# One weight load of a spectral transformer block, issued by ScalarE in the third group of the frequency stage instead of by SyncE

## The chip, the core and the metric

The kernel runs on one core of a Trainium2 chip. The core has a matrix engine (TensorE, PE in the profile; its weight loads are listed as PEld), a vector engine (VectorE, DVE), a scalar engine (ScalarE, ACT), a general engine (GpSimd, POOL) and a sequencer without arithmetic (SyncE, SP). Each works through its own list of instructions in order, and semaphores tie the lists together. Any of SP, ACT and POOL can issue a DMA; the transfer itself runs on 16 DMA engines and ends with a semaphore. The metric is the time of one execution in microseconds of device time. Shown is the median of several runs.

## What is computed

A block of 2048 tokens of width 640 with conditioning: a layer norm, scaled and shifted by parts of a modulation vector, goes through a two-dimensional Fourier filter; a second layer norm, scaled and shifted by other parts, goes through a gated feed-forward layer.

```python
mod = (_silu(c) @ w_mod).reshape(c.shape[0], 6, 1, -1)
sa, ca, ga, sb, cb, gb = (mod[:, 0].copy(), mod[:, 1].copy(), ...)
h = _layernorm(x, axis=-1) * (1 + ca) + sa
x = x + ga * _A_ref(h, A_w_r, A_w_i)          # rfft2, times (w_r + i w_i), irfft2
h = _layernorm(x, axis=-1) * (1 + cb) + sb
x = x + gb * _B_ref(h, B_w_gate, B_w_up, B_w_down)   # (silu(h Wg) * (h Wu)) Wd
```

`w_mod` has 640 rows and six column blocks of 640. The blocks for `sb` and `cb`, the shift and the scale of the second layer norm, are what this document is about: 1600 KB together.

## The kernel before

The order of the work on every engine is the order in which the program issues it; nothing is rearranged. Four parts follow one another.

First, to about 36 us, the tokens are transformed along the width and half way along the sequence, in 16 tiles of 128 tokens. In this part SP has some 20 loads in its list, the filter weights and their mirrored copies among them. Of `w_mod`, the blocks `ca` (L247, L249), `sa` (L275) and `ga` (L279) are loaded here.

Second comes the frequency stage, from about 37 to 63 us. The 81 kept frequencies of the width are worked on in 21 groups (`NG`) of two to four. For a group g,

- `stage_a(g)` makes one TensorE matmul for each frequency (L567) into two banks of PSUM, and VectorE multiplies the result by the filter weights in two instructions (L592, in `prod`);
- `stage_b(g)` sums the products with matmuls against the identity (L599) into bank 0 or 1, and ScalarE copies that bank out (L602);
- `stage_c(u)`, two or three groups later, transforms back (L620), and `evac` moves two groups' results out at a time, most of them by ScalarE (L637). GpSimd then makes a turned copy (L648).

The loop over g (L694) runs `stage_a(g + 2)`, `stage_b(g)` and `stage_c` of the unit that is due, in this order. The frequencies reach `stage_a` transposed. The first 18 (groups 0 to 4) are transposed by TensorE (`t2_pe`, L538). The others come by four DMA transposes (`t2_dma`, L519), issued by SP one after the other: for groups 5 to 8, 9 to 12, 13 to 16 and 17 to 20. Before the first group of such a batch is used, GpSimd adds a constant to it (`sa_add`, L559).

Right behind the four transposes, SP's list has the load of the blocks `sb` and `cb` (L527), the block `gb` (L528), two tables for the inverse transform (H, L529, and RI, L530), and the weights of the feed-forward layer from L734 on. In `w_mod`'s tile they are `wm_r[:, :, 1:3, :]` and `wm_r[:, :, 3, :]`.

What reads `sb` and `cb` is `mod_col` (L578 to L581): five matmuls of one output column each for one of the five 128-wide pieces of the width. They are strewn into `stage_a` of the last four groups, 17 to 20, behind the first matmul of the group (L568 to L570): two pieces in groups 17 and 18, three in 19 and 20. Each engine's list being in order, the other matmuls of these groups stand behind them. `gb` is read at the end of the stage (L718).

Third, to about 82 us, the inverse transform along the sequence and the width, with the residual and the statistics of the second norm (L669, L678, L1184 to L1189). It reads H and, scaled by `ga`, RI (L724, L728).

Fourth, the feed-forward layer in four chunks of tokens, from 82 us to the end (gate and up: L1013 and L1043; down: L891 and L914).

A DMA issue here also waits for the last DMA that used the same one of eight semaphores. For L527 that is the load of a table at L280, about 20 us earlier.

Of the kernel before, what the change touches and what calls it, by code (L numbers as in the profile page):

```python
# [149 lines left out]
def _rev(ap, free_off, dims):  # L150
    a = ap[:]
    return bass.AP(tensor=a.tensor, offset=a.offset + free_off, ap=[list(a.ap[0])] + [list(d) for d in dims])
# [3 lines left out]
def adaln_block_kernel(ctx, tc, A_x, A_w_r, A_w_i, B_x, B_w_gate, B_w_up, B_w_down, c, w_mod, out):  # L156
    nc = tc.nc
# [55 lines left out]
    wm_r = rM.cut(12800, [NC5, 4, D])  # L213
# [19 lines left out]
    def banks(b, n, shape=None, dt=F32):  # L233
        ap = psum[:, b:b + n, :].rearrange("p b e -> p (b e)")
        if dt == BF16:
            ap = ap.bitcast(BF16)
        if shape is not None:
            ap = ap[:, 0:int(np.prod(shape))]
            if len(shape) > 1:
                ap = ap.rearrange("p (a b) -> p a b", a=shape[0])  # L240
        return ap
# [36 lines left out]
    wm_m = wm_v[:, :, 2 * D:6 * D].rearrange("p k (i d) -> p k i d", i=4)  # L278
# [46 lines left out]
    if True:  # L325
# [76 lines left out]
        def wsum(W, lo, hi, eng):  # L402

            off = lo if W is Wn else NW - hi
            v = [_rev(W, NT * NW * i + off, [[NW, NT], [160, 2], [1, hi - lo]]) if W is Wn else
                 _rev(W, NT * NW * i + off - 160, [[NW, NT], [160, 2], [1, hi - lo]]) for i in range(3)]
            eng.tensor_tensor(v[1], v[2], v[0], ALU.add)
# [104 lines left out]
    if True:  # L512
        B2of = {}

        def t2_dma(bi):
            l0 = (1, 16, 32, 64)[bi]
            n = 15 if bi == 0 else 16
            B2b = rL.cut(4096 * bi, [16, 128]) if bi < 3 else rM.cut(6144, [16, 128])
            nc.sync.dma_start_transpose(B2b[:, :n, :], A_sb[:, l0:l0 + n, :, :, :].rearrange("p l t c r -> p l (t c r)"))  # L519
            for i in range(n):  # L520
                B2of[l0 + i] = (B2b, i, l0, n)
# [2 lines left out]
        t2_dma(1)  # L524
        t2_dma(2)
        t2_dma(3)
        nc.sync.dma_start(wm_r[:, :, 1:3, :], wm_m[:, :, 1:3, :])  # L527
        nc.sync.dma_start(wm_r[:, :, 3, :], wm_m[:, :, 3, :])  # L528
        nc.sync.dma_start(Htab[:], H_dram)  # L529
        nc.sync.dma_start(RI[:], RI_dram)  # L530
# [22 lines left out]
        def sa_add(g):  # L553
            if g < 5 or g >= NG:
                return
            B2b, i, l0, nb = B2of[groups[g][0]]
            if l0 not in seen:
                seen.add(l0)
                nc.gpsimd.tensor_tensor(B2b[:, :nb, 0:1], B2b[:, :nb, 0:1], SA[:, l0:l0 + nb].unsqueeze(2), ALU.add)  # L559

        def stage_a(g):
            ls = groups[g]
            n = len(ls)
            xps = banks(6 if g == 2 else 2 + 2 * (g % 2), 2, [4, 256])
            for i, l in enumerate(ls):
                B2, j = B2of[l][0:2]
                nc.tensor.matmul(xps[:, i, 0:192], lhsT=B2[:, j, :], rhs=KS2, start=True, stop=True)  # L567
                if i == 0:  # L568
                    for c5 in {NG - 4: (0, 1), NG - 3: (0, 1), NG - 2: (2, 3, 4), NG - 1: (2, 3, 4)}.get(g, ()):
                        mod_col(psum[:, 2 + 2 * (g % 2), 192 + c5:193 + c5], wm_r[:, :, 1 + g % 2], c5)  # L570
            PP = rM.cut(1536 * (g % 4), [3, 2, NT, 2, n])
            prod(g, PP, xps, 0)
            if g == 0:
                wsum(Wv, 48, 64, nc.vector)
            prod(g, PP, xps, 1)
            return PP

        def mod_col(o, w, c5):  # L578
            for k in range(NC5):
                nc.tensor.matmul(o, lhsT=w[:, k, 128 * c5:128 * c5 + 128], rhs=sc_col[:, k:k + 1],  # L580
                                 start=(k == 0), stop=(k == NC5 - 1))  # L581
# [12 lines left out]
        def stage_b(g, PP):  # L594
            n = len(groups[g])
            yps = banks((g + 1) % 2, 1, [4, 128])
            for ps in (1, 0):
                for i in range(n):
                    nc.tensor.matmul(yps[:, i, :], lhsT=_rev(PP, 64 * n * ps + i, [[n, 128]]), rhs=identb[:],  # L599
                                     start=(ps == 1 and i == 0), stop=(ps == 0 and i == n - 1))  # L600
            Y2 = rY.cut(1024 * (g % 4), [4, 128])
            nc.scalar.copy(Y2[:, 0:n, :], yps[:, 0:n, :])  # L602
            return Y2
# [8 lines left out]
        def stage_c(u):  # L612
            for g in units[u]:
                ls = groups[g]
                n, l0 = len(ls), ls[0]
                eps_ = banks({NG - 4: 4, NG - 3: 5, NG - 2: 0, NG - 1: 1}.get(g, 6 + (l0 // 4) % 2), 1, [4, 128])
                Y2 = Y2s.pop(g)
                for i, l in enumerate(ls):
                    kv = {0: 1, 80: 2}.get(l, 0)
                    nc.tensor.matmul(eps_[:, i + 4 - n if l0 else i, :], lhsT=Y2[:, i, :], rhs=Ktab[:, 128 * kv:128 * kv + 128],  # L620
                                     start=True, stop=True)

        def evac(u):
            g, l0 = units[u][0], groups[units[u][0]][0]
            if l0 == 0:
                edge = rY.cut(4096, [2, 128])
                nc.scalar.copy(edge[:], banks(6, 1, [4, 128])[:, 0:2, :])
                for i in range(2):
                    nc.gpsimd.tensor_copy(Em[:, :, :, 64 * i].rearrange("p v q -> p q v"),
                                          edge[:, i, :].rearrange("p (q v) -> p q v", v=2))  # L630
            elif g == NG - 2:
                nc.vector.tensor_copy(ep_views(l0, 4), banks(0, 1, [4, 128]).rearrange("p i q -> p q i"))
            elif g == NG - 1:
                nc.scalar.copy(ep_views(l0, 4), banks(1, 1, [4, 128]).rearrange("p i q -> p q i"))
            else:
                n = len(groups[g]) + 4
                (nc.vector.tensor_copy if g == NG - 6 else nc.scalar.copy)(  # L637
                    ep_views(l0, n), banks(4 if g == NG - 4 else 6, 2, [8, 128])[:, 8 - n:8, :].rearrange("p i q -> p q i"))
                if g < NG - 4:
                    rots.extend((l0, n, i) for i in range(0 if g == NG - 6 else 2))  # L640

        def rot(l0, n, qs, eng, ops=(0, 1)):
            if l0 < 64:
                E0, E1 = (Em[:, v].rearrange("p q (c j) -> p q c j", c=2)[:, qs, :, l0:l0 + n] for v in range(2))
            else:
                E0, E1 = (Er[:, v, qs, :, l0 - 64:l0 - 64 + n] for v in range(2))
            for i in ops:
                eng.tensor_scalar(E1[:, :, 1 - i, :], E0[:, :, i, :], 1.0 - 2.0 * i, 1.0, ALU.mult, ALU.mult)  # L648
# [45 lines left out]
        for g in range(NG + 1):  # L694
            if g > 1:
                sa_add(g + 4)
            for W, lo, hi in {0: ((Wv, 80, 81), (Wv, 0, 16)), 1: ((Wv, 16, 32),), 3: ((Wv, 32, 48),), 11: ((Wn, 64, 80),), 13: ((Wv, 64, 80),)}.get(g, ()):
                wsum(W, lo, hi, nc.gpsimd)
                if g == 0 and hi == 81:
                    sa_add(5)  # L700
            if 0 < g < NG - 2:
                PPs[g + 2] = stage_a(g + 2)
            if g == NG - 3:
                nc.vector.tensor_copy(modcols[:, 2, :], psum[:, 2, 192:197])
                nc.vector.tensor_scalar_add(one_p_cb[:], psum[:, 4, 192:197], 1.0)
            if rots:
                l0, n, i = rots.pop(0)
                rot(l0, n, slice(0, 64), nc.gpsimd, (i,))
            if g < NG:
                Y2s[g] = stage_b(g, PPs.pop(g))  # L710
            for u, gs in enumerate(units):
                if gs[-1] + (1 if gs[0] >= NG - 2 else 3 if gs[0] == 4 else 2) == g:
                    stage_c(u)
                    evac(u)
            if g == NG - 3:
                rot(40, 8, slice(0, 64), nc.vector)
            if g == NG - 1:
                for c5 in range(NC5):  # L718
                    mod_col(psum[:, 3, 192 + c5:193 + c5], wm_r[:, :, 3], c5)
# [602 lines left out]
```

## Time and profile before

| | |
|---|---|
| median of 3 runs | 248.64 us (248.44 to 250.56) |
| the profiled execution | 249.31 us, of which the span is 247.5 |
| granted TensorE clock | 1.00 |
| first part, 0 to 37 us: PE busy | 35.53 us |
| frequency stage, 37 to 63 us: PE, DVE, ACT busy | 24.97, 23.05, 21.62 us |
| inverse transform, 63 to 82 us: PE, DVE, ACT busy | 18.98, 16.94, 16.97 us |
| load of `sb` and `cb` (L527): issue, landing | 48.06 us, 7.3 us later |

The span is the time from the first to the last instruction of the profiled execution; the rest of its time lies around it. Busy times are those of instructions; the issue of a DMA is listed on the engine's sequencer (SPq, ACTq) and is not counted as busy. The number in brackets behind a line of a timeline is the idle time of the engine before it, and what ended it. Where several like instructions were merged into one row, the row gives their count and the time from the first one's start to the last one's end.

### The profile page before, as it was taken

The numbers are of one execution on the slowest core, as the hardware profiler recorded it, in microseconds if no ns is written. First come the engines' busy times: TensorE is split into PE (matmuls) and PEld (weight loads), VectorE is DVE, ScalarE is ACT, GpSimd is POOL, SyncE is SP. The second block draws the span as 40 slices with busy tenths as digits, with TensorE's granted clock in tenths as the row PEclk, the third lists the DMA queues.
The fourth block names the chain that finished last, engine by engine and source line by source line (L and its number), as shares of the span: only waits on it lengthen the run. The fifth ranks groups of instructions, "written<-read, shape, count | busy, mean of one in ns | idle before, by whom it ended". The sixth has DMA issues, their size and how long they took to land.

```text
span 247.5 us, 6173 instructions
## 1 busy us (share of the span) xinstructions
PE 241.5 (98%) x2327; PEld 189.7 (77%) x2327; DVE 207.7 (84%) x516; ACT 167.8 (68%) x327; POOL 78.1 (32%) x128
## 2 busy tenths in 40 slices
PE   8999999999999999999999999999999999999994
PEld 3778877989999888688887778887765666656773
DVE  3799699988898998789989977788998787789864
ACT  3778757996989698489774488866246777773220
POOL 8577765993243605002004400000432000004400
PEclk9999999999999999999999999999999999999999
DMA  7999999999999999600005110200411000000111
GB/s 220 396 361 315 307 391 177 179 337 392 295 348 317 298 280 187 139 15 3 0 3 106 53 55 3 57 0 19 93 49 53 3 0 1 4 0 0 53 56 53
DMA packets 45760, 34.74 MB, mean 140 GB/s; under 512 B 21732, under 2 KB 42659, under 8 KB 45347
## 3 DMA queue, kind: packets, MB, share of 16 engines
q1 hardware_dynamic: 43936, 30.00, 42.7%
q0 software_dynamic: 1504, 4.28, 7.4%
q8 instruction: 18, 0.29, 0.5%
q10 hardware_dynamic: 290, 0.08, 0.1%
q14 instruction: 12, 0.09, 0.1%
HBM read 27.05 MB, written 4.72 MB: 128 GB/s over the span
## 4 chain that ended last, share of the span: by engine, by line
PE 89%; DVE 4%; DMA 3%; issue 1%; ACT 0%; POOL 0%; DVEq 0%; SPq 0%; ACTq 0%; POOLq 0%
PE psum L1043 36%; PE psum L914 19%; PE psum L1013 6%; PE psum L891 3%; DMA rM<-in_w_mod_dram 3%; PE psum L669 3%; PE psum L599 2%; PE psum L296 2%; PE psum L1184 2%; PE psum L1187 2%; PE psum L1001 2%; PE psum L567 2%; DVE rE L382 2%; PE psum L318 1%; PE psum L315 1%; PE psum L393 1%
## 5 line engine op out<-in xcount | busy, mean ns | idle before, releaser
L1043 PEld LDWEIGHTS <-rW 128*128 128x128 bf16 (+1 forms) x429 | 42.0, 98 | 12.6
L1043 PE MATMUL psum<-rW 128*128 128x256 bf16 (+1 forms) x247 | 42.2, 287 | 0.0
L940 POOL TENSOR_TENSOR rM<-rM,rL 128x320 f32<-128x320 f32 x6 | 5.4, 906 | 96.6 <-ACT rL L939 96.6
L914 PEld LDWEIGHTS <-rE 128*128 128x128 f16 (+1 forms) x196 | 19.0, 97 | 7.8
L914 PE MATMUL psum<-rE 128*128 128x320 f16 (+1 forms) x147 | 22.9, 299 | 0.0
L592 DVE TENSOR_TENSOR rM<-psum,rW 128x384 bf16<-128x384 f32 (+2 forms) x42 | 20.2, 543 | 2.7 <-PE psum L567 1.2
L1074 ACT COPY rH<-psum 128x384 f32<-128x384 f32 (+2 forms) x27 | 14.0, 517 | 7.4 <-PE psum L1043 6.0
L1081 ACT COPY rX<-psum 128x384 f32<-128x384 f32 (+2 forms) x27 | 14.0, 520 | 7.2 <-PE psum L1043 7.0
L1043 PEld LDWEIGHTS <-rE 128*128 128x128 f16 x156 | 15.3, 98 | 4.7
L1078 DVE TENSOR_TENSOR rH<-psum,rM 128x512 bf16<-128x512 f32 (+1 forms) x24 | 15.0, 624 | 4.4 <-PE psum L1043 2.2
L1097 ACT ACTIVATE rL<-psum 128x384 bf16<-128x384 f32 (+2 forms) x27 | 14.4, 533 | 5.3 <-PE psum L1043 3.4
L1082 DVE TENSOR_TENSOR rX<-psum,rX 128x384 f32<-128x384 f32 (+2 forms) x27 | 16.3, 604 | 1.6 <-ACT rX L1081 1.4
L1068 ACT COPY rM<-psum 128x384 f32<-128x384 f32 (+2 forms) x27 | 13.9, 516 | 4.2 <-PE psum L1043 4.2
L382 DVE SCALAR_TENSOR_TENSOR rE<-rE,mv,psum 128x648 bf16<-128x648 f32 (+1 forms) x17 | 14.2, 840 | 2.1 <-PE psum L318 1.7
L1043 PE MATMUL psum<-rW,rE 128*128 128x256 bf16 (+1 forms) x78 | 15.6, 290 | 0.0
L1043 PE MATMUL psum<-rE,rY 128*128 128x256 f16 (+1 forms) x78 | 15.6, 290 | 0.0
L338 ACT COPY rE<-psum 128x640 bf16<-128x640 bf16 x16 | 11.1, 693 | 6.1 <-PE psum L336 5.1
L1098 ACT ACTIVATE rL<-rX 128x384 bf16<-128x384 f32 (+2 forms) x27 | 15.1, 559 | 0.0
L1013 PE MATMUL psum<-rW 128*128 128x256 bf16 x130 | 14.5, 272 | 0.0
L602 ACT CAST rY<-psum 128x512 bf16<-128x512 f32 (+2 forms) x21 | 11.8, 574 | 3.9 <-PE psum L599 3.6
L1189 DVE SCALAR_TENSOR_TENSOR rM<-psum,rX 128x640 f32<-128x640 f32 x16 | 13.0, 820 | 1.7 <-PE psum L1187 1.6
L883 DVE TENSOR_TENSOR rA<-psum,rM 128x320 bf16<-128x320 f32 (+1 forms) x27 | 12.1, 472 | 2.4 <-PE psum L891 2.3
(223 smaller groups left out, 666.5 us busy)
## 6 DMA issues: line engine op xcount, KB each, us to landing
out_dram<-rA SPq DMA_DIRECT2D x31, 80.0 KB, 1.6
rM<-in_w_mod_dram SPq DMA_DIRECT2D x3, 800.0 KB, 10.2
rX<-in_A_x_dram SPq DMA_DIRECT2D x3, 640.0 KB, 7.4
rA<-in_B_w_down_dram SPq DMA_DIRECT2D x2, 960.0 KB, 14.4
rY<-in_B_w_gate_dram POOLq DMA_DIRECT2D x2, 832.0 KB, 7.9
rM<-in_w_mod_dram SPq DMA_DIRECT2D x1, 1600.0 KB, 7.3
rW<-in_B_w_gate_dram SPq DMA_DIRECT2D x2, 640.0 KB, 7.1
rW<-in_B_w_up_dram SPq DMA_DIRECT2D x2, 640.0 KB, 7.1
```

The lines of the kernel that those rows point to most:

```text
L382: nc.vector.scalar_tensor_tensor(Zv[:, h], Cv[:, h], mv[:, t, 0:1], zps[:, h], ALU.mult, ALU.subtract)
L592: nc.vector.tensor_tensor(PP[:, :, hl], xv[:, :, hl], in1, ALU.mult)
L914: nc.tensor.matmul(o, lhsT=lhs[rows(k), k], rhs=rhs[rows(k), k], start=start and k == ks[0], stop=stop and k == ks[-1], skip_group_check=True)
L1013: nc.tensor.matmul(gu[u], lhsT=Wgu[:, u, c5, ff * 128:(ff + 1) * 128], rhs=h2T[:, :, c5, :], start=(c5 == 0), stop=(c5 == NC5 - 1))
L1043: nc.tensor.matmul(o[:, f], lhsT=w, rhs=b, start=(start and f == 0 and i == 0), stop=(stop and f == len(groups[g]) - 1 and i == len(ops) - ...
L1068: nc.scalar.copy(c0, X)
L1074: nc.scalar.copy(c2, X)
L1078: nc.vector.tensor_tensor(c11, Z, c0, ALU.add)
L1081: nc.scalar.copy(c3, X)
L1082: nc.vector.tensor_tensor(c22, Y, c3, ALU.add)
L1097: nc.scalar.activation(g21, X, ACT.Silu, scale=-1.0)
L1098: nc.scalar.activation(g22, c22, ACT.Silu, scale=-1.0)
```

## The change

The load of the two blocks `sb` and `cb` is taken out of SP's list. ScalarE issues it, in the loop over the groups, at g = 2: behind its copy of group 2's sum (L602 of before) and ahead of its copy of group 3's. The transfer, its source, its destination and the semaphore that it waits for and signals are the same. On PE, VectorE and GpSimd no instruction is added, removed or moved. On ScalarE, one later instruction (the first square of the second norm) no longer lists a wait for this load's semaphore. Lines behind L527 have numbers one lower in the changed kernel up to the new statement, and one higher behind it.

```diff
         t2_dma(1)
         t2_dma(2)
         t2_dma(3)
-        nc.sync.dma_start(wm_r[:, :, 1:3, :], wm_m[:, :, 1:3, :])
         nc.sync.dma_start(wm_r[:, :, 3, :], wm_m[:, :, 3, :])
         nc.sync.dma_start(Htab[:], H_dram)
         nc.sync.dma_start(RI[:], RI_dram)
...
             if g < NG:
                 Y2s[g] = stage_b(g, PPs.pop(g))
+                if g == 2:
+                    nc.scalar.dma_start(wm_r[:, :, 1:3, :], wm_m[:, :, 1:3, :])
             for u, gs in enumerate(units):
                 if gs[-1] + (1 if gs[0] >= NG - 2 else 3 if gs[0] == 4 else 2) == g:
                     stage_c(u)
```

## The prediction

> **What bounds the kernel now.** I read the page first, then the chain of waits in order of time, then the timelines of PE, DVE, SP and ACT around the change, and last the busy table in half-microsecond stretches. The page's first part:
>
> ```profile
> PE 241.5 (98%) x2327; PEld 189.7 (77%) x2327; DVE 207.7 (84%) x516; ACT 167.8 (68%) x327; POOL 78.1 (32%) x128
> ```
>
> PE is busy in 98% of the span at a granted clock of 1.000, so only a hole in PE can be won. From 63 us on the table of stages shows PE full (18.98 of 19, 22.00 of 22, 40.00 of 40), so a gain before 63 us moves everything behind it, and so does a loss. The chain, cut to 36 to 66 us (start, length, what):
>
> ```profile
> 47.29 0.59 ACT rY L602
> ...
> 48.06 7.32 DMA rM<-in_w_mod_dram
> 55.38 0.05 issue
> 55.43 0.40 PE psum L580 x10
> ```
>
> The load that the change moves (L527) is itself a link: issued at 48.06, landed at 55.38, and 0.05 us later PE starts the ten one-column products that read it. The timelines of PE and DVE there (start, busy time, line, shape, count, idle before):
>
> ```profile
> 54.59 0.25 PE L567 MATMUL psum<-Ktab,rM 128*128 128x192 bf16 x1
> 55.43 0.40 PE L580 MATMUL psum<-sc_col,rM 128*128 128x1 bf16 x10 [0.59 <-DMA rM<-in_w_mod_dram]
> ```
>
> ```profile
> 53.59 1.48 DVE L592 TENSOR_TENSOR rM<-psum,rW 128x384 bf16<-128x384 f32 x3
> 56.19 1.99 DVE L592 TENSOR_TENSOR rM<-psum,rW 128x384 bf16<-128x384 f32 x4 [1.12 <-issue]
> ```
>
> PE has one matmul of group 17 done and then stands still; the three others of the group wait behind L580 in program order, and DVE, which had worked without a gap, is idle for 1.12 us. Next, what SP did before it came to L527:
>
> ```profile
> 37.10 7.00 SPq L519 DMA_TRANSPOSE rL<-rA  x3
> 44.21 3.81 SPq L519 DMA_TRANSPOSE rM<-rA  x1
> 48.06 0.59 SPq L527 DMA_DIRECT2D rM<-in_w_mod_dram  x1
> 48.70 0.52 SPq L528 DMA_DIRECT2D rM<-in_w_mod_dram  x1
> 49.26 0.52 SPq L529 DMA_DIRECT2D rH<-tab_H  x1
> ```
>
> L527 stands behind four transposes that hold SP for 10.9 us. Taken one by one they are issued at 37.10, 38.86, 41.64 and 44.21 and the first, third and fourth land 4.3, 5.7 and 5.2 us later, at 41.4, 47.3 and 49.4; for the second the trace gives no landing. ACT, which is to issue the load now:
>
> ```profile
> 40.67 0.59 ACT L602 CAST rY<-psum 128x512 bf16<-128x512 f32 x1 [0.35 <-PE psum L599]
> 41.63 1.22 ACT L602 CAST rY<-psum 128x512 bf16<-128x512 f32 x2 [0.37 <-PE psum L599]
> 43.46 0.59 ACT L602 CAST rY<-psum 128x512 bf16<-128x512 f32 x1 [0.61 <-PE psum L599]
> 43.97 1.01 ACT L637 CAST rE<-psum 128x1024 bf16<-128x1024 f32 x1
> ```
>
> The first line is group 0's copy, the second those of groups 1 and 2, which end at 42.85; group 3's starts at 43.46 after 0.61 us of idle time. The new issue falls into this gap. Last, the DMA engines (the last two columns are their busy share and GB/s):
>
> ```profile
> 44.00:44.50 0.50, 0.50 (x10) 0.50 (x8) 0.42 (x2) 0.50 (x2) 0.50 (x1) 1.00 1.64 237
> ...
> 45.00:45.50 0.50, 0.50 (x10) 0.46 (x9) 0.50 (x2) 0.50 (x2) 0.48 (x2) 1.00 0.06 6
> 45.50:46.00 0.50, 0.50 (x11) 0.50 (x9) 0.50 (x2) 0.46 (x2) 0.50 (x3) 1.00 0.08 10
> 46.00:46.50 0.50, 0.50 (x11) 0.50 (x9) 0.50 (x2) 0.50 (x1) 0.49 (x1) 1.00 1.14 254
> ```
>
> Between the third and the fourth transpose almost nothing moves, and while they run it is 200 to 290 GB/s, against some 400 from 51 us on. There is room for a load.
>
> **The change part by part.**
>
> *Out of SP.* One issue of 0.59 us goes, so the loads behind it (L528, the H and RI tables) are issued 0.64 us earlier (48.70 less 48.06), and 1600 KB no longer lie ahead of them. Nobody waits for them now: H lands at 61.46 (49.26 + 12.2) and is first read at 63.03; RI lands at 62.2 (49.83 + 12.4) and DVE touches it at 63.32. Even at their old landing times they would be in time for readers that come 0.76 us sooner (62.27, 62.56). Worth nothing by itself.
>
> *Into ACT.* The same issue on ACT. Three rows price it: 0.59 us for this very transfer on SP, and 0.53, 0.35 and 0.35 us for ACT's own three DMA issues (L244, L248, L884). I take 0.59, the same transfer; it fits the gap of 0.61. The new instruction waits only for the last DMA on its semaphore, the table load L280, issued at 27.56 and landed 5.9 us later, long before. Queued behind it are group 3's copy and all of ACT's copies and evacuations. Without the cover the most this form costs is the whole 0.59 us. That would not be made up: from 49 to 55 us a pair of groups takes 2.0 us on PE, DVE and ACT alike (2.00, 1.95 and 1.99 busy of 2.00 in 51 to 53). An evacuation ends at 51.90 (50.88 + 1.02) and PE overwrites its banks at 52.14, so about 0.24 us of a delay would be swallowed and 0.35 passed on. No row shows an ACT issue while SP is issuing a transpose; below, that is the unknown cost: nothing at the low end, and up to the end of SP's fourth transpose at 48.02 at the high end. I take nothing, because at the start of the program ACT's L248 (1.3 us) took 0.35 us while SP was issuing too.
>
> *The load itself.* Issued at 42.85 instead of 48.06, 5.2 us earlier. Its old 7.32 us would bring it at 50.2; PE wants it at 54.67 (54.59 plus 0.08 for one L567 matmul). It has 4.5 us in hand. What it meets on the engines is the tail of the third transpose and the fourth one, 0.52 MB at 200 to 290 GB/s, or 2 to 2.5 us. It is still in time after these.
>
> *The stall.* L580 starts at 54.67 instead of 55.43: 0.76 us. DVE's next product follows L580 and the three L567 by 0.76 us (55.43 to 56.19), so it comes at 55.43 instead; DVE is free at 55.07, so it gives the whole 0.76. ACT ends its evacuation at 55.90 and would copy group 15 at 55.90, not 56.64: 0.74. What is late next is PE itself: with 10, 10, 15 and 15 extra products in these four groups, it is full in 57 to 63. The last part of w_mod (L528) is read at 62.18 and landed at 58.9, so it doesn't take the place of the stall.
>
> Sum: +0 for ACT's issue, 0 for SP's, -0.76 for the stall. The profiled execution took 249.31 us (span 247.5 and 1.8 around it) and would take 248.55. The median of the three runs is 248.64, 0.67 below the profiled one, so 247.9.
>
> **The rivals.**
>
> *ACT is held by SP's transposes (slower).* SP needed 3.81 us to issue the fourth transpose, and its release at 48.02 comes 0.7 us after the third had landed: an issuer can be held by what is still queued. If ACT's issue at 42.85 must queue behind the transposes, there are two points. Behind the third alone (44.10) it ends at 44.69, group 3's copy is 1.23 us late, and less the slack of 0.24 and the stall of 0.76 that is +0.2: 248.9. Behind the fourth (48.02) it ends at 48.61, group 3's copy is 5.15 us late, and the same subtraction gives +4.15: 252.8. It eats into the gain from an issue of 0.85 us on (0.61 gap and 0.24 slack) and is a loss from 1.6 us on (0.76 more). For it: SP's own blocked issues (5.67 us at L273, 7.30 at L736). Against: those were held by SP's own queue (q1 on the page), and ACT's (q10, 0.1% of the engines' time) is empty.
>
> *The transposes come late.* The load's 1.6 MB at 400 GB/s are 4.1 us of engine time, put before the tail of the third transpose if it is unlucky. That would land at 51.4 instead of 47.3; POOL adds to it (0.27 us) and PE reads it as group 13 at 50.59: 1.1 us late, less 0.76 is +0.3, or 249.0. At the worst that the page shows for a queued transfer (10.7 us, L275, against the transpose's 5.7) it lands at 52.3: 2.0 late, +1.25, 249.9. The fourth has 3.8 us to spare (49.4, added to at 53.16), so it hardly decides. Against: at 44.5 the third's data have almost all moved. The Trainium skill's page "DMA: Bandwidth & Descriptors", section "Issuing engines are not separate DMA queues", speaks against the change here: transfers issued from different engines run on the same 16 engines and interleave, and a second issuer saves only issue time, usually small. By that rule alone the sum would be no gain and this rival's loss; the trace adds the idle stretch at 45 to 46 us, which the rule doesn't weigh.
>
> *No change.* The change does not do what it says if the new queue's data wait until the transposes are through at 48.5: then 1.6 MB at half the rate of 400 GB/s, beside SP's next loads, take 8 us and land at 56.5, 1.1 us later than now; at the whole rate they land at 52.5, in time; midway is the landing of now. Or ACT's 0.59 us are not covered, and 0.35 of them come off the gain. Between +1.1 and -0.4, nearest to nothing: 248.6.
>
> **How the numbers follow.** Forecast (stall gone, issue hidden): 0.56. ACT held to the third transpose: 0.10; to the fourth: 0.14. Transposes late: 0.08. No change: 0.12. Predicted: 247.9. The range's low end is DVE's whole gap of 1.12 us won, less 0.2 for the spread of the two nearer runs (248.44, 248.64): 247.3. Its high end is the worst of the late transposes, 249.9 and the same 0.2: 250.1. Left out are ACT held to the end (0.14) and 0.03 below. A change under 1% (2.5 us) is about what a measurement of this kernel cannot tell from none. Faster by over 1% has no case in the profile, as the only hole is 1.12 us: 0.02 for what I don't see. Slower by over 1% is ACT held to the fourth, with 0.02 more: 0.16. The rest, 0.82, is within.
>
> **What would show it.** Right: ACT's issue at about 42.9 taking under 0.6 us, group 3's copy starting within 0.1 us of 43.46, no wait of L580 for the load, L580 first at about 54.7, and the H stage's first L669 at 62.3 instead of 63.03. ACT held: a long DMA issue on ACT and idle time of PE in L599 or L620 at 43 to 49. Transposes late: POOL's L559, now L558, waiting for the DMA into rL, with PE's group 9 or 13 behind it. No change: L580 still waiting, or a new gap of the same size ahead of it. The forecast is wrong if any of these stands where the 0.76 us were.

## The result and the profile after

The changed kernel takes 251.27 us (median of 14 runs, 250.14 to 253.59), the kernel before on the same chip 249.58 us (14 runs, 248.44 to 251.19). The ratio is 1.007, with a 95% interval of 1.0048 to 1.0093: about 1.7 us slower. The profiled execution took 251.66 us, 249.9 of them span. Single executions over 1.5% slower than the fastest of the same kernel are left out of all ratios below, and the profiles of two experiments (two fifths on ACT; between the transposes, reordered) were taken in such executions, so their times show little.

The first part of the page, busy time by engine:

```profile
PE 241.0 (96%) x2327; PEld 189.2 (76%) x2327; DVE 208.1 (83%) x516; ACT 167.7 (67%) x327; POOL 77.7 (31%) x128
```

The work is the same as before; the share of PE fell from 98 to 96% because the span grew. So a new hole in PE is what to look for. The timeline of PE (start, busy time, line, shape, count; in brackets the idle time before and what ended it):

```profile
53.69 0.50 PE L566 MATMUL psum<-Ktab,rL 128*128 128x192 bf16 x4 [2.56 <-POOL rL L558]
...
57.70 0.25 PE L566 MATMUL psum<-Ktab,rM 128*128 128x192 bf16 x1
57.78 0.39 PE L579 MATMUL psum<-sc_col,rM 128*128 128x1 bf16 x10
```

The old stall is gone: the column products (L579 now) follow the matmul ahead of them at once. A hole of 2.56 us stands four groups earlier, ahead of group 13, the first that reads the third transpose. The timelines of DVE and POOL show the same place:

```profile
54.23 3.95 DVE L591 TENSOR_TENSOR rM<-psum,rW 128x384 bf16<-128x384 f32 x8 [2.77 <-PE psum L566]
```

```profile
53.37 0.27 POOL L558 TENSOR_TENSOR rL<-rL,SA 128x16 bf16<-128x16 bf16 x1 [3.27 <-DMA rL<-rA]
```

DVE waits for PE, PE for POOL's addition, POOL for the third transpose. The chain of waits in order of time (start, length, what) names the transfer and its length:

```profile
42.16 11.14 DMA rL<-rA
53.29 0.07 issue
53.37 0.28 POOL rL L558
53.64 0.05 issue
53.69 0.50 PE psum L566 x4
```

The third transpose landed 11.1 us after its issue; before it was 5.7. SP felt it as well, in its own timeline:

```profile
37.52 7.10 SPq L519 DMA_TRANSPOSE rL<-rA  x3
44.72 8.32 SPq L519 DMA_TRANSPOSE rM<-rA  x1
53.09 0.59 SPq L527 DMA_DIRECT2D rM<-in_w_mod_dram  x1
```

The fourth transpose held SP for 8.32 us instead of 3.81 and was released only when the third had nearly landed. The moved issue itself, on ACT's timeline:

```profile
42.02 1.22 ACT L601 CAST rY<-psum 128x512 bf16<-128x512 f32 x2 [0.34 <-PE psum L598]
42.66 0.40 ACTq L711 DMA_DIRECT2D rM<-in_w_mod_dram  x1
43.85 0.58 ACT L601 CAST rY<-psum 128x512 bf16<-128x512 f32 x1 [0.61 <-PE psum L598]
```

It took 0.40 us, from 42.66 to 43.06, while the copy of group 2 was still running (to 43.24). So it was over before the gap began, and the copy behind it waited 0.61 us for PE's sum, exactly as before. What the load did to the transposes is in the table of DMA queues. q10 is ACT's queue with the load (2560 bytes a packet), q1 is SP's with the transposes (256 bytes a packet); the columns are packets, MB and the share of the 16 engines' time. First the kernel after, from 49 to 50 us, then the kernel before, from 47 to 48 us:

```profile
q10 hardware_dynamic: 143, 0.37, 92.2%
q1 hardware_dynamic: 143, 0.04, 16.1%
```

```profile
q1 hardware_dynamic: 1132, 0.29, 127.4%
```

In this microsecond the engines move one packet of the load for each one of the transposes: 143 and 143. In each tenth of it either queue moves 10 to 16 packets, never more than there are engines, so the turns are of single packets. The transposes get 0.04 MB in a microsecond instead of 0.29. Other microseconds of the same execution say the same (86 and 87 from 46 to 47, 111 and 112 from 48 to 49); only in the load's first and last microseconds do the transposes move more (54 and 142 from 45 to 46, 99 and 314 from 51 to 52). When the load is through, from 52 us on, the transposes run at 856 packets in a microsecond again.

The balance: PE's hole of 2.56 us less the 0.59 us of idle time that the old stall cost it is 1.97, beside the 1.7 between the medians. The first part happened to end 0.42 us later in this execution (SP's first transpose is issued at 37.52, before at 37.10). Together that is 2.39, and the H stage's first product (L668) starts 2.35 us later, at 65.38 instead of 63.03. From there the two traces run alike to the end: the spans differ by 2.4.

### The profile page after: what moved, and what is told of

It is laid out like the page before. It is cut to its first block, busy times and chain, and to the rows that moved or that the text cites. A ratio compares the mean times of both kernels' runs of the same rounds, so it can differ in the third digit from the quotient of the medians.

```text
span 249.9 us, 6172 instructions
## 1 busy us (share of the span) xinstructions
PE 241.0 (96%) x2327; PEld 189.2 (76%) x2327; DVE 208.1 (83%) x516; ACT 167.7 (67%) x327; POOL 77.7 (31%) x128
## 4 chain that ended last, share of the span: by engine, by line
PE 84%; DMA 7%; DVE 5%; SPq 2%; issue 1%; ACT 1%; POOL 0%; DVEq 0%; ACTq 0%
PE psum L1044 36%; PE psum L915 19%; PE psum L1014 6%; DMA rL<-rA 4%; PE psum L892 3%; PE psum L668 3%; DMA rM<-in_w_mod_dram 2%; PE psum L598 2%; PE psum L1002 2%; PE psum L1185 2%; PE psum L1188 2%; SPq L519 1%; DVE rE L382 1%; PE psum L318 1%; PE psum L315 1%; PE psum L393 1%
## 5 line engine op out<-in xcount | busy, mean ns | idle before, releaser
L338 ACT COPY rE<-psum 128x640 bf16<-128x640 bf16 x16 | 11.1, 694 | 5.8 <-PE psum L336 4.7
## 6 DMA issues: line engine op xcount, KB each, us to landing
rM<-in_w_mod_dram ACTq DMA_DIRECT2D x1, 1600.0 KB, 10.1
```

## The experiments

Ratios are to the kernel before on the same chip, with 12 or 13 runs of the experiment against 29 or 35 of the kernel before. "Landing" is the time from issue to the end of a transfer in the profiled execution. Three causes were set against each other, called P, B and C in the expectations. P: the two queues take turns by packets, so small packets lose to large ones. B: the load's bytes as such go ahead of the third transpose. C: the issue on a second queue, or its number of descriptors, holds the transposes.

**The same bytes in packets of half the size.** Two loads of one block each take the place of the one.

```diff
                 if g == 2:
-                    nc.scalar.dma_start(wm_r[:, :, 1:3, :], wm_m[:, :, 1:3, :])
+                    for i in (2, 1):
+                        nc.scalar.dma_start(wm_r[:, :, i, :], wm_m[:, :, i, :])
```

> The moved load is cut into two on ACT, block by block, both issued at group 2: the same bytes in twice as many packets of half the size. Theory P (packets of the two queues go one for one, so each small packet of the third transpose waits for one large one): about 860 small packets, 54 for each engine, are still to go, so 54 x 1280 B stand before the last instead of 40 x 2560 B, two thirds. The third transpose lands about 9 us after its issue instead of 11.1, POOL's wait for it falls from 3.3 to about 1 us, ratio to before 0.998 to 1.003. Theory B (the bytes of the load come first whatever their packets): 11.1 us again, wait 3.3 us, ratio 1.007. Theory C (ACT's issue holds SP's work on its transposes): two issues hold it longer, over 11.1 us, ratio 1.007 to 1.010.

Measured: 1.0056 (1.0025 to 1.0087). The third transpose landed after 9.4 us, against 11.1 in the changed kernel. Timeline of POOL and PE, and the queues from 49 to 50 us:

```profile
52.09 0.27 POOL L558 TENSOR_TENSOR rL<-rL,SA 128x16 bf16<-128x16 bf16 x1 [1.35 <-DMA rL<-rA]
```

```profile
52.41 0.50 PE L566 MATMUL psum<-Ktab,rL 128*128 128x192 bf16 x4 [0.64 <-POOL rL L558]
```

```profile
q10 hardware_dynamic: 248, 0.30, 82.6%
q1 hardware_dynamic: 250, 0.06, 28.4%
```

The turns are again one for one, now with 1280-byte packets, and the transposes get 250 packets in a microsecond instead of 143. PE's hole fell from 2.56 to 0.64 us. That the bytes are equal and the delay is not speaks for P, and the counts speak against B: the load's bytes do not go ahead, they alternate with the transposes. These are readings of one execution each; the times alone do not tell P from B, as 1.007 lies within the interval. P's own time was missed: 0.998 to 1.003 would have gone with so small a hole. The profiled execution, 250.35 us, lies 1.0 us below the median of these runs, so it shows only a part of the loss. In it DVE also waited 1.0 us for the filter weights at the stage's start; the kernel with the small load, below, has the same wait and loses nothing. Where the rest of the loss lies stays open.

**The load when the third transpose is through.** As the changed kernel, but in the sixth group.

```diff
-                if g == 2:
+                if g == 5:
                     nc.scalar.dma_start(wm_r[:, :, 1:3, :], wm_m[:, :, 1:3, :])
```

> The load is issued on ACT at group 5 instead of 2, about 3 us later (45.6 to 46), when the third transpose has hardly a packet left. P and B: the third transpose lands 5.7 to 6.5 us after its issue, POOL doesn't wait for it, PE's group 13 has no gap; the fourth is now the one that is mixed, lands about 9 us after its issue (at 53.5 to 54, where 53.2 to 54.6 would do), and the load lands at 54 to 55.5, so that little or nothing is left of either stall: ratio 0.997 to 1.002. C: the fourth transpose's issue is what is held, and its landing comes late by the same 5 us as the third's did, past 55; ratio 1.003 to 1.008.

Measured: 0.9995 (0.9964 to 1.0025), and 1.0009 (0.9985 to 1.0034) when repeated. SP's, ACT's and POOL's timelines:

```profile
44.19 3.47 SPq L519 DMA_TRANSPOSE rM<-rA  x1
```

```profile
45.42 0.42 ACTq L711 DMA_DIRECT2D rM<-in_w_mod_dram  x1
```

```profile
49.45 0.61 POOL L558 TENSOR_TENSOR rL<-rL,SA 128x16 bf16<-128x16 bf16 x1
53.81 0.27 POOL L558 TENSOR_TENSOR rM<-rM,SA 128x16 bf16<-128x16 bf16 x1 [0.36 <-DMA rM<-rA]
```

The third transpose landed after 5.5 us and nobody waited for it. Now the fourth pays: it landed after 9.6 us instead of 5.2, with 139 packets of each queue in the microsecond from 50 to 51. It has room for that: POOL waited 0.36 us and PE not at all. The same issue on the same queue, 2.8 us later, does no harm, and SP's issue of the fourth took 3.47 us, no longer than before. That speaks against C; the small load, below, settles it.

**The load between the third and the fourth transpose, in SP's own queue.**

```diff
         t2_dma(2)
-        t2_dma(3)
         nc.sync.dma_start(wm_r[:, :, 1:3, :], wm_m[:, :, 1:3, :])
+        t2_dma(3)
```

> The load on SP again, but ahead of the fourth transpose instead of behind it: one queue, so nothing is mixed. P: the third transpose is untouched (5.7 us), POOL doesn't wait at group 13; the load is issued at about 44.2, lands at 51 to 52, no stall at L580; the fourth transpose lands about 4 us later than before, at 53.5, where POOL wants it at 53.2 and PE at 54.6. Ratio 0.996 to 0.999. B: the same, since its bytes stand behind the third here. If the fourth is later than 54.3, PE waits at group 17 for POOL instead of for the load and the ratio is 1.000 or above.

Measured: 0.9987 (0.9966 to 1.0008). In one queue the transfers keep their order: the load, issued at 44.12, landed after 7.7 us, the third transpose ahead of it after 5.5 as ever, the fourth behind it after 8.4 (45.16 to 53.56; added to at 53.60). No reader of the third or the fourth waits, nor do the column products.

**A load of 60 KB with just as many descriptors.** The kernel before, with a second load on ACT in the third group: 640 packets of 96 bytes into a part of the buffer that nobody reads then.

```diff
                 Y2s[g] = stage_b(g, PPs.pop(g))
+                if g == 2:
+                    nc.scalar.dma_start(rM.cut(40448, [NC5, 48]), wm_m[:, :, 1, 0:48])
```

> The kernel before with SP's L527 in its place, and one more load on ACT at group 2: 640 packets, as many as the moved load has, but of 96 B instead of 2560 B (60 KB), into a scratch space that nobody reads. P: 40 more packets for each engine stand among the third transpose's, each as short as its own (about 20 ns), so it lands 6 to 6.7 us after its issue instead of 5.7; POOL wouldn't wait, PE's group 13 has no gap, L580's wait stays at 0.6 to 0.8 us. Ratio 0.999 to 1.002. C (the issue on ACT, or making its 640 descriptors, holds SP's transposes): the same number of descriptors, so the third lands 10 to 11 us after its issue, SP's fourth issue takes about 8 us, ratio 1.007 or more (both stalls).

Measured: 0.9999 (0.9978 to 1.0020). The list of DMA issues from 36 to 60 us (KB each, us to landing):

```profile
rM<-in_w_mod_dram ACTq DMA_DIRECT2D x1, 60.0 KB, 4.8
rL<-rA SPq DMA_TRANSPOSE x3, 5.5
rM<-rA SPq DMA_TRANSPOSE x1, 5.3
```

The 5.5 is a median over the transposes into `rL`; the third and the fourth landed after 5.7 and 5.3 us. ACT's issue took 0.40 us here too. The same place, the same queue and 640 packets again, but small ones: no delay. So neither the issue nor the number of descriptors holds the transposes, and C falls. This load also has fewer bytes, so alone it does not tell length from bytes; with the halves above, where the bytes were equal, and the counts, it is the length of the packet that the transposes have to let pass.

**Two fifths of the load on ACT, three fifths in SP's old place.**

```diff
-        nc.sync.dma_start(wm_r[:, :, 1:3, :], wm_m[:, :, 1:3, :])
+        nc.sync.dma_start(wm_r[:, 2:5, 1:3, :], wm_m[:, 2:5, 1:3, :])
...
+                if g == 2:
+                    nc.scalar.dma_start(wm_r[:, 0:2, 1:3, :], wm_m[:, 0:2, 1:3, :])
```

> Two of the five row blocks of the load (256 packets of 2560 B, 16 for each engine) on ACT at group 2, the other three on SP in the old place of L527. P: 16 x about 0.1 us come before the third transpose's last packets: it lands 7.3 to 7.7 us after its issue instead of 11.1, at about 49.5, where POOL wants it at 49.2 and PE at 50.6: no gap of PE above 0.2 us. The 960 KB on SP land at 53.5 to 54, so L580 doesn't wait. Stage 0.6 to 0.8 us shorter than before. C or a fixed price of a second queue: 10 to 11 us again, PE's gap at group 13 2 to 2.6 us. What the stage wins may be lost at the first chunk's gate and up weights' product (L1001), which waits for POOL and the transpose of the second norm: ratio 0.997 to 1.003.

Measured: 1.0014 (0.9992 to 1.0035). The third landed after 8.1 us, a little above what P had given (7.3 to 7.7). PE had no gap at group 13, but another wait came that was not expected:

```profile
57.72 0.38 PE L580 MATMUL psum<-sc_col,rM 128*128 128x1 bf16 x8 [2.60 <-DMA rM<-in_w_mod_dram]
```

The first three transposes held SP for 9.74 us in this execution, the three fifths were issued only at 50.87 and landed at 57.7 instead of 53.5 to 54.

**The load in two halves, both in SP's old place.** This takes the stall away without a second queue and without touching the transposes.

```diff
-        nc.sync.dma_start(wm_r[:, :, 1:3, :], wm_m[:, :, 1:3, :])
+        for i in (2, 1):
+            nc.sync.dma_start(wm_r[:, :, i, :], wm_m[:, :, i, :])
```

> The kernel before, but L527 as two loads on SP in its old place, the block of group 17 first. All theories: the transposes land as before (5.7 and 5.2 us). The first block's 800 KB land about 2 us sooner than 55.4, at 53 to 53.5, the second at 55.4 to 55.9, where group 18 wants it at 55.7. L580's wait of 0.6 to 0.8 us goes, at most 0.2 comes back at group 18. Ratio 0.997 (0.995 to 0.999). If something else is late right behind the stall: 1.000.

Measured: 1.0059 (1.0028 to 1.0089), and 1.0028 (1.0001 to 1.0055) when repeated. The halves landed after 5.6 and 7.1 us, the column products did not wait, and the H stage began at 62.6 instead of 63.0. But the gain did not reach the end. POOL's and PE's timelines at the first chunk of the feed-forward layer, where POOL scales the transposed tokens (L798) and PE reads them (L1002):

```profile
80.14 2.48 POOL L798 TENSOR_SCALAR rW<-rW,one_p_cb,modcols 128x256 bf16<-128x256 bf16 x4 [9.55 <-DMA rW<-rL]
```

```profile
81.60 0.27 PE L1002 MATMUL psum<-rW,Wp 128*128 128x256 bf16 x1 [0.59 <-POOL rW L798]
```

In the kernel before, POOL's line starts at 78.22 and PE's first such product at 80.79, without a wait. Here the transpose of that chunk landed 8.2 us after its issue instead of 5.8, and PE stood still for 1.5 us in four pieces. The repeat shows that this is not the whole of it: its profiled execution has no wait there (the transpose landed after 6.2 us; PE stood still for 1.3 us at the stage's start instead, behind DVE and the filter weights), and its runs are still slower than before, if only just by the interval. Why this version loses stays open.

**The wait at the first chunk.** Two edits were tried against it. One moves the first load that POOL issues for the feed-forward layer from the ninth tile of the inverse transform to its first tile, ahead of that transpose:

```diff
+                gu_dma(GS[0][:], B_w_gate, 0, 2, True)
...
-            if t in (8, 11):
-                gu_dma(GS[0][:], B_w_gate, t // 11 * 2, 2, t == 8)
+            if t == 11:
+                gu_dma(GS[0][:], B_w_gate, 2, 2, False)
```

With the halves:

> e3 (the load as two on SP) with POOL's first accumulating weight load issued at the start of the inverse transform (66.2 us) instead of at tile 8 (69.7 us). Theory M: e3's loss is the same mixing at the other end: the transpose for the first feed-forward chunk (1280 packets of 256 B, issued at 71.7) has POOL's 3328-B packets between its own and stands behind SP's loads, lands 8.2 us after its issue, and PE's L1002 waits 1.5 us for POOL. With POOL's load through by 74 to 75, the transpose lands 5 to 6.5 us after its issue, L1002 waits under 0.4 us, ratio 0.996 to 1.000. If e3's loss has another cause (its queue on SP is simply 0.6 us longer): 8 us again and 1.004 to 1.008.

With the load between the transposes:

> e4 (the load on SP ahead of the fourth transpose) with POOL's first accumulating weight load early, as in e7. The stage as in e4 (about 0.4 to 0.7 us shorter than before), L1001 without a wait, so that what the stage wins is kept: ratio 0.996 to 0.999. If POOL's earlier load only delays SP's loads ahead of the transpose by as much as it frees, the transpose lands at the same time and the ratio is e4's, 0.9987.

Measured: 1.0036 (1.0016 to 1.0055) and 1.0051 (1.0022 to 1.0080), both missed. With the halves, the transpose did land after 4.7 us and PE did not wait for POOL. The waits from 60 to 90 us (us in total, times, longest) show the price:

```profile
DVE rL L776 <- POOL rstd L772: 1.3, 1, 1.3
PE psum L1185 <- DVE rM L1190: 1.1, 1, 1.1
```

The issue stands ahead of the first standard deviations in POOL's list, so DVE waited for these, PE for DVE, and the transpose was issued at 73.23 instead of 71.73. In the second kernel the first three transposes happened to hold SP for 9.40 us, the fourth, behind the load, landed after 10.2, and PE met it:

```profile
57.48 0.26 PE L567 MATMUL psum<-Ktab,rM 128*128 128x192 bf16 x1 [2.27 <-POOL rM L559]
```

So the room of the fourth transpose is not always enough. The other edit moves one of SP's weight loads from ahead of the chunk's transpose to behind it:

```diff
-    load_gu(512, 1024, (0,))
...
-                load_gu(512, 1024, (1,))
+                load_gu(512, 1024)
```

It was run alone, with the halves, with the load in the sixth group (twice) and with the load between the transposes.

> Control: the kernel before with one of SP's later loads (the gate weights' columns 512 to 1024, 640 KB, issued at 68.4) moved behind the transpose for the first feed-forward chunk (72.2). That transpose no longer queues behind 640 KB (1.6 us at 400 GB/s), lands 1 to 2 us sooner, but PE didn't wait for it (L1001 followed the last matmul of tile 15). All theories: L580's stall stays, the ratio is 0.999 to 1.001.

> e3 (two loads on SP in the old place) with the same reordering. Theory M (what e3 won in the frequency stage was lost where PE waits for the transpose of the first feed-forward chunk, landed 8.2 us after its issue): the transpose lands at 76 to 78.5 instead of 79.9, L1002 waits under 0.5 us instead of 1.5, and the 0.5 us won in the frequency stage is kept: ratio 0.997 to 1.000. If e3 is slow for another reason: 1.004 to 1.008 again.

> e2 (the load on ACT at group 5) with the same reordering. P and M: stage 0.3 to 0.7 us shorter than before as in e2, the fourth transpose mixed but in time, L1002 without e2's wait of 0.6 us: ratio 0.996 to 0.999. Otherwise e2's 0.9995.

> e4 (the load on SP ahead of the fourth transpose) with the same reordering. e4 had no wait at L1001, so the reordering adds nothing: the ratio is e4's, 0.9966 to 1.0008, nearest 0.998. If the fourth transpose lands over 9 us after its issue in some executions, as in e8, the ratio is 1.000 or above.

> e11 again, on another chip or at another time, as the only version so far whose interval lies below the kernel before. If the frequency stage's 0.5 us are kept: ratio 0.996 to 0.999, L1001 without a wait for POOL above 0.3 us. If e11 was the luck of its executions: 0.999 to 1.002.

> e3 again. Theory M: whatever the transposes of the frequency stage do in this execution, PE's wait for POOL at L1002 comes back (0.5 to 2 us) and takes what L580 gives: ratio 1.002 to 1.007. If e3's 1.0059 belonged to its executions: 0.998 to 1.001 and no wait at L1002.

> e2 again, beside e13 on the same chip: the same without the reordering. M: a wait of 0.3 to 1 us at L1002, ratio above e13's by 0.001 to 0.003, 0.998 to 1.001. If the reordering does nothing: the same ratio as e13.

Measured, in this order: alone 0.9997 (0.9964 to 1.0030); halves 1.0001 (0.9970 to 1.0032); sixth group 0.9968 (0.9938 to 0.9998); between the transposes 0.9991 (0.9965 to 1.0017); sixth group again 0.9996 (0.9966 to 1.0025). The last two texts are for the plain repeats given above. In the profiled executions of the sixth group PE does not wait at the first chunk (0.6 us in the plain version, 0.2 in its repeat), and the spans are 247.3 and 247.2 us. With the halves the wait stayed (1.0 us, the transpose landed after 7.8 us), so its time was just above the expected range of 0.997 to 1.000, and its mechanism was missed. Between the transposes a wait of 1.7 us stands at the first chunk, where none was expected. The gain of the sixth group, once 0.3%, was not repeated. No version is shown to beat the kernel before.

## Why the prediction was wrong, step by step

- *What bounds the kernel*: right. PE is the bound, and the time went where PE got a hole.
- *Out of SP*: worth nothing, as said, though for another reason. The loads behind it were issued 4.4 us later than before, not 0.64 earlier (L527 at 53.09 instead of 48.70), and no reader waited for them.
- *Into ACT*: hidden, as said. It took 0.40 us instead of the 0.59 assumed, and it did not need the gap: ACT's sequencer issued it beside the running copy. The rival of an ACT held by SP's transposes, with a chance of 0.24 in two parts, is refuted: 0.40 us here, 0.42 in the sixth group, 0.40 for the small load and 1.04 for the two halves, all beside SP's transposes.
- *The load itself*: in time, as said. It landed at 52.8 (10.1 us after its issue; 9.3 to 9.8 had been allowed) and was needed at 57.78. But the 0.52 MB that it was said to meet are the fourth transpose alone, 2048 packets of 256 bytes; the third's tail is not in the figure.
- *The stall*: gone, as said.
- *What is late next*: here the forecast failed. It named PE itself; it was the third transpose. The sentence that did it stands against the rival of late transposes: "at 44.5 the third's data have almost all moved". Counted in packets, the first three transposes have 6016 (15, 16 and 16 frequencies of 128 packets); the queue had moved some 5070 of them by 44.5 and 5150 by 45.0 in the trace of before. About 870 of the third's 2048 were still to come then. The idle stretch from 45 to 46 us, read as room for a load, was a pause in the middle of that transpose and not its end, as the queue of the kernel before shows from 44 to 45, 45 to 46 and 46 to 47 us:

```profile
q1 hardware_dynamic: 487, 0.12, 248.1%
q1 hardware_dynamic: 30, 0.01, 7.1%
q1 hardware_dynamic: 1081, 0.27, 120.8%
```

So the sum put the delay of the third transpose at nothing. In the profile after, some 1500 of its packets were to come when the load's first one moved, at 44.5. The load's 640 packets, 40 for each engine at 0.103 us (92.2% of 16 engines for 143 packets), found enough of them to take turns with all: 4.1 us, by this estimate. The measured delay was 5.4. The load's first 149 packets needed 2.5 us, from 44.5 to 47.0, where 0.103 us would make 1.0; why they were so slow is not shown.
- *The rival of late transposes* had the mechanism right ("put before the tail of the third transpose if it is unlucky") and even these 4.1 us, but took them as bad luck at 0.08. With such turns they follow, by this count, for any load of 640 packets of 2560 bytes that meets the third transpose with as many or more to go. Its price of +1.25 at the worst stands against a measured 1.7.
- *The numbers*: 247.9 hung on the median of three runs, 248.64; 14 runs give 249.58. The upper end of 250.1 was built on the same base. Of the 1.17 us from 250.1 to 251.27, 0.94 is this base.
- *"A gain before 63 us moves everything behind it"*: not shown to hold. A loss did move everything. Where the repaired versions reach the H stage earlier, it is by 0.15 to 0.5 us, and some of these profiles show a part coming back as PE's wait at the first chunk, where the kernel before has 0.07 us between POOL's end and PE's start. But the reordered kernel without any change to the load reached the H stage 0.65 us later than the kernel before, so a gain of this size cannot be told from chance in single profiles.

The Trainium skill's page "DMA: Bandwidth & Descriptors", section "Issuing engines are not separate DMA queues", which the prediction weighed against its trace, was borne out: the transfers interleaved, and nothing was saved. The Trainium skill's same page, section "Queues, rings and completion order", says how: each DMA engine goes round the queues that have work, one packet at a time. The traces agree, with 143 and 143, 248 and 250 packets in a microsecond. The Trainium skill gives some 9 to 17 descriptors for a typical packet there; here the turns were single pieces of 256 and 2560 bytes, as the counts by tenths of a microsecond show.

## What to carry to other kernels

In this kernel a second queue was not a second set of DMA engines: what it carried took turns, packet by packet, with what was already moving, and a load in packets of 2560 bytes slowed a transfer in packets of 256 (here a transpose) from 1132 to 143 of them in a microsecond. Before an issue is moved earlier, count in packets what is still to come of every transfer in flight, and ask who reads that first; an idle stretch of the engines does not say that a transfer is done. A transfer that must jump ahead can be put into the same queue behind the urgent one, or issued when that one is through: here both left the third transpose alone, though neither made the kernel faster than before.

## What was not expected of the hardware

In every trace of this case, the data all but stop for about 1 us in the midst of the transposes: 30 packets from 45 to 46 us before, 16 from 47 to 48 after, 106 from 45 to 47 with the halves and the reordered load. The cause was not found. The first three transposes held SP for 6.99 to 9.46 us in kernels that do the same up to there, and DVE waited 0 to 1.7 us for the filter weights at the stage's start. A difference of less than about 1 us in one profiled execution is therefore not yet an effect of the edit.
